# Attention ahead of two expert layers: blocks of 128 queries with both heads in turn, side work and copies from a table, routing scratch in SBUF, first operands piece by piece

## The chip, the cores and the metric

The kernel runs on one core of one Trainium2 chip. The metric is the device time in microseconds (us) of one execution; the median of three runs is given. The engines are named as in the profile: PE (TensorE; PEld is its weight load), DVE (VectorE), ACT (ScalarE), POOL (GpSimd), SP (SyncE, which here issues transfers).

## What is computed

The reference, cut: an attention in which a query sees only keys of the same hash bucket, a layer of eight experts of which each token takes two, and a dense layer.

```python
B, H, S, D = 2, 8, 768, 64
q_bucket = sum(((q @ proj) > 0) * 2 ** arange(6)); k_bucket = likewise
scores = where(q_bucket == k_bucket, q @ k.T / 8, -1e9)
x = softmax(scores) @ v                       # -> 1536 tokens x 512
noisy = x @ w_gate + log1p(exp(x @ w_noise)) * noise
two largest of noisy per token -> experts, weights = softmax of the two
out[token] += weight * (relu(x[token] @ w1[e]) @ w2[e])      # 8 experts, 512 -> 1024 -> 512
h = out @ w_in;  result = (h * sigmoid(1.702 * h)) @ w_out   # 512 -> 2048 -> 512
```

## The kernel before

Three stages follow each other: attention (with the routing of tokens worked in), the experts, the dense layer. The change touches the attention alone, which ends about where `f_tr` (L830) begins, 272.8 us into the span.

**Blocks.** Attention is 96 steps g. A step is one block of 128 queries of one head against all 768 keys. Six steps make a unit u (two heads j, three blocks c of 384 queries), two units a pair of heads n. `dec(g)` says which block a step is: up to unit 14, three blocks of head 0 and then three of head 1. A step's work is: `a_score` (L298, four matmuls into a tile s, two buffers), `a_soft` (L310 to L312, DVE takes the row maximum), `a_exp` (L321, ACT writes P), `a_trans` (L340, six PE transposes into two tiles p, then two copies p to PT, L269 on ACT or L275 on DVE), `a_av` (L351, P times V into the PSUM bank av), `a_x` (copy of av to xu) and `a_xt` (L385, L388 and the DVE operations L380 to L395: the scaled rows of tokens and the router's logits). The loop writes the score of step g+2, then the transposes of step g, then the exponential of step g+2, then a piece of `a_av` for the unit before, then the side work of the step. Every engine takes its instructions in this written order.

**Side work.** The operands of a pair of heads (u1, v1, u2, v2: a rounded part and a rest of q and k, with hash bits as extra rows) are made ahead: `a_load` (SP), `a_hash` (L191), `a_hb` (L206, L207), `a_split` (ACT L180, L185; rest on POOL, L182, L186), `a_bits` (POOL transfers). `w_load` and `w_conv` bring six weight tiles of the experts (ACT L721, POOL L729). `r_do` runs the routing of 384 tokens in small DVE operations (L429 to L486), `r_scatter` (L493, L494) writes their rows to expert order with two indirect transfers on POOL per 128 tokens. `at(g, f)` and `at_m` put each at a step by rule (every unit, every eighth step, the next free step); for the first pair `z_q`, `z_k`, `z_hash` make all operands of a head before its first score.

**What else the change touches.** `copy` chooses ACT or DVE by the running loads `la` and `ld`. The routing keeps lg, v and w0 in columns 392 to 488 of the PSUM bank av (`pt`, and `iotp`). PT of head 0 lies in two buffers of its own (PT0), that of head 1 in hh and hl, which the experts use later. The raw q and k have one buffer each. `WARM` matmuls of ones (L523) run before the first data are there.

## Time and profile before

| | |
|---|---|
| median of 3 runs | 878.44 us (878.43 to 879.76) |
| the profiled execution's own time | 880.22 us |
| its span, first to last instruction | 878.5 us |
| PE busy | 849.7 us (97%) |
| DVE, ACT, POOL busy | 528.2, 441.8, 218.4 us |
| mean granted TensorE clock | 0.996 |

The span is what the trace shows; what lies around it (1.7 us) is only in the execution's time. PE's busy time is modelled from pipelined matmuls, whose records overlap, so that a busy PE can still wait; the distance from one matmul's start to the next says more.

### The profile page before, as it was taken

Reading aid. Unit: us, or ns where it says so; the run is one execution under the profiler, and the core shown is the slowest. Engines: PE = TensorE matmul, PEld = TensorE weight load, DVE = VectorE, ACT = ScalarE, POOL = GpSimd, SP = SyncE. Lnnn points to the kernel's source line nnn. Section 1 sums busy time; section 2 is a strip of 40 time slices with the busy share of each in tenths; the row PEclk is TensorE's granted clock in tenths of the full one; section 3 lists DMA queues with packets and bytes.
Section 4 is the critical chain, followed back from the end, with each engine's and each line's share of the span. In section 5 each row is a group of like instructions: output and inputs, shape, how many; then the busy total and the mean of one; then the engine's idle time right before and its main releaser. Section 6 shows DMA issues by size and latency. Waiting matters only on the chain.

```text
span 878.5 us, 14095 instructions
## 1 busy us (share of the span) xinstructions
PE 849.7 (97%) x5409; PEld 740.5 (84%) x5409; DVE 528.2 (60%) x1082; ACT 441.8 (50%) x782; POOL 218.4 (25%) x226
## 2 busy tenths in 40 slices
PE   7899999989998999999999999999999999999997
PEld 5567666666667999999999999988899898989897
DVE  6876777877575588989898898748512121212120
ACT  5787888777663444444545443448523131414130
POOL 5241554386122100000000000006614151504040
PEclk9999999999999999999999999999999999999999
DMA  3746644573126667878878686649301010010000
GB/s 100 251 140 203 191 127 136 163 205 79 62 90 210 232 206 230 275 253 277 253 250 298 208 286 211 207 146 334 98 25 49 25 42 31 27 47 1 25 1 27
DMA packets 52376, 132.20 MB, mean 150 GB/s; under 512 B 8912, under 2 KB 11024, under 8 KB 52304
## 3 DMA queue, kind: packets, MB, share of 16 engines
q1 hardware_dynamic: 43488, 108.82, 38.1%
q0 software_dynamic: 6992, 20.37, 7.5%
q10 hardware_dynamic: 1824, 2.05, 0.8%
q8 instruction: 44, 0.72, 0.3%
q14 instruction: 28, 0.23, 0.1%
HBM read 92.05 MB, written 35.39 MB: 145 GB/s over the span
## 4 chain that ended last, share of the span: by engine, by line
PE 87%; DVE 6%; ACT 4%; DMA 1%; issue 1%; another core or an unknown queue 0%; SPq 0%; ACTq 0%; DVEq 0%
PE av L351 7%; PE s L298 6%; PE y L875 5%; PE y L877 5%; PE y L876 5%; PE g L1109 5%; PE g L1108 5%; PE g L1110 5%; PE h L851 5%; PE h L852 5%; PE h L853 5%; PE p L340 5%; PE o L1156 4%; PE o L1154 4%; PE o L1155 4%; DVE mx L310 2%
## 5 line engine op out<-in xcount | busy, mean ns | idle before, releaser
L1118 POOL TENSOR_TENSOR gl<-sg,gh 128x512 fp32r<-128x512 f32 x48 | 67.3, 1402 | 162.3 <-ACT gh L1117 162.3
L321 ACT ACTIVATE P<-s,sm 128x768 f32<-128x768 f32 x96 | 95.2, 992 | 21.9 <-DVE sm L312 16.4
L310 DVE TENSOR_REDUCE mx<-s 128x1 f32<-128x768 f32 x96 | 91.5, 953 | 20.7 <-PE s L298 20.1
L1063 POOL DMA_INDIRECT yg<-ys,ysl x24 | 24.7, 1031 | 303.9 <-issue 302.2
L298 PE MATMUL s<-v,u 76*128 76x384 f32 (+1 forms) x384 | 93.3, 365 | 5.2 <-ACT P L321 3.8
L340 PE MATMUL p<-ident,P 128*128 128x128 f32 x576 | 82.9, 278 | 7.9 <-ACT PT L269 3.2
L298 PEld LDWEIGHTS s<-v,u 76*128 76x128 f32 (+1 forms) x384 | 63.0, 191 | 30.5 <-issue 13.0
L1114 DVE TENSOR_TENSOR sg<-g,sg 128x512 f32<-128x512 f32 x48 | 33.2, 691 | 91.4 <-ACT sg L1113 87.1
L340 PEld LDWEIGHTS p<-ident,P 128*128 128x128 f32 x576 | 67.6, 141 | 18.4 <-ACT PT L269 5.6
L351 PE MATMUL av<-PT,v 128*64 128x384 f32 (+1 forms) x216 | 73.6, 470 | 2.0 <-DVE rw L431 1.5
L858 ACT ACTIVATE hh<-h 128x416 fp32r<-128x416 f32 x56 | 29.0, 518 | 72.8 <-PE h L853 72.3
L875 PE MATMUL y<-hh,wh 128*128 128x416 f32 (+1 forms) x144 | 51.2, 356 | 0.0
L877 PE MATMUL y<-hh,wl 128*128 128x416 f32 (+1 forms) x144 | 49.9, 346 | 0.0
L876 PE MATMUL y<-hl,wh 128*128 128x416 f32 (+1 forms) x144 | 49.8, 346 | 0.0
L1113 ACT ACTIVATE sg<-g 128x512 f32<-128x512 f32 x48 | 28.7, 598 | 39.5 <-PE g L1110 37.1
L351 PEld LDWEIGHTS av<-PT,v 128*64 128x64 f32 x216 | 25.9, 141 | 26.8 <-issue 22.3
L1117 ACT ACTIVATE gh<-sg 128x512 fp32r<-128x512 f32 x48 | 30.3, 630 | 31.1 <-DVE sg L1114 30.3
L269 ACT ACTIVATE PT<-p 128x384 f32<-128x384 f32 x75 | 33.3, 486 | 19.5 <-PE p L340 16.9
L859 DVE SCALAR_TENSOR_TENSOR hl<-h,hh 128x416 fp32r<-128x416 f32 x56 | 32.9, 588 | 14.2 <-ACT hh L858 14.1
L1108 PE MATMUL g<-x2h,wh 128*128 128x256 f32 x144 | 40.1, 278 | 0.7 <-ACT x2h L1092 0.7
L1109 PE MATMUL g<-x2l,wh 128*128 128x256 f32 x144 | 40.1, 278 | 0.3 <-DVE x2l L1093 0.3
L1109 PE MATMUL g<-btl,wh 128*128 128x256 f32 x144 | 40.2, 279 | 0.0
(334 smaller groups left out, 2548.2 us busy)
## 6 DMA issues: line engine op xcount, KB each, us to landing
ws<-in_w SPq DMA_DIRECT2D x40, 512.0 KB, 4.9
d_in<-in_w SPq DMA_DIRECT2D x32, 512.0 KB, 4.9
bth<-in_w SPq DMA_DIRECT2D x16, 512.0 KB, 6.3
btl<-in_w SPq DMA_DIRECT2D x16, 512.0 KB, 4.2
wd<-d_o SPq DMA_DIRECT2D x32, 256.0 KB, 3.6
xs<-xeh SPq DMA_DIRECT2D x13, 512.0 KB, 6.8
rawk<-in_kT SPq DMA_DIRECT2D x15, 384.0 KB, 5.0
rawq<-in_qT SPq DMA_DIRECT2D x14, 384.0 KB, 3.8
```

The source lines that it names most:

```text
L298: nc.tensor.matmul(ps[:, hf, :HALF], l[:kk, q0:q0 + 128], r[:kk, hf * HALF:(hf + 1) * HALF], start=st, stop=not st)
L310: nc.vector.tensor_reduce(mx, ps[:, :, :HALF], axis=AX.XY, op=ALU.max, negate=True)
L321: nc.scalar.activation(P, ps[:, :, :HALF], AF.Exp, bias=sm[:, 1:2], scale=sm[:, 0:1], accum_out=self.RS[u][:, c, j, 0:1])
L340: nc.tensor.transpose(ps[:, kb, :], P[:, hf, kb * 128:(kb + 1) * 128], self.ident)
L351: nc.tensor.matmul(self.AV[u, c][64 * j:64 * j + 64, :], self.vt[n][:, kb, 64 * j:64 * j + 64], self.PT[u, j][:, kb, cs], start=(kb == 0), ...
L851: nc.tensor.matmul(ps, wh[:, fs], xh[:, d, :n], start=(d == 0), stop=False)
L875: nc.tensor.matmul(ps, wh[:, ds_], hh[:, f, :], start=(f == 0), stop=False)
L876: nc.tensor.matmul(ps, wh[:, ds_], hl[:, f, :], start=False, stop=False)
L877: nc.tensor.matmul(ps, wl[:, ds_], hh[:, f, :], start=False, stop=(f == 7))
L1108: nc.tensor.matmul(ps[:, x, :], wh[:, fs], xh[:, d, :], start=(d == 0), stop=False)
L1109: nc.tensor.matmul(ps[:, x, :], wh[:, fs], xl[:, d, :], start=False, stop=False)
L1118: nc.gpsimd.tensor_tensor(gl[:, fo, :], g, gh[:, fo, :].bitcast(F32), op=ALU.subtract)
```

## The change

- `dec` takes the two heads of a block in turn (unit 0 has an order of its own), and `a_av` multiplies one block of 128 queries as soon as both heads are transposed: at steps 3 and 5, then at each even step. Before, it took 384 queries of both heads, two of six key blocks at a time, in the unit after. PT is now one block of both heads, alternately in hh and hl; PT0 is gone, and the raw q and k have two buffers.
- Each piece of side work has its step in a table written out; each copy has its engine in the string `COPIES` (151 on ACT and 59 on DVE, where it was 145 and 65).
- The routing's lg, v and w0 are SBUF tiles; two copies that were there to bring an operand out of PSUM or into it are gone.
- The first pair's operands are made by eight small functions from the table, the loads of k come earlier, the rest of head 0's keys (v2) is made on POOL, and 27 warm-up matmuls run instead of 40.

The diff, cut to its core (the table has some 190 rows):

```diff
-WARM = 40
+WARM = 27
...
         if n == 0:
+            raw = {(nm, j): self.t(self.ap, [128, S], F32, f"raw{nm}{j}", 2) for j in range(2) for nm in ("q", "k")}
+            nc.scalar.dma_start(raw["k", 0], a["kT"][b, 2 * p])
             nc.scalar.dma_start(self.projq, a["projq"])
-            raw = {(nm, j): self.t(self.ap, [128, S], F32, f"raw{nm}{j}", 1) for j in range(2) for nm in ("q", "k")}
-            nc.scalar.dma_start(raw["k", 0], a["kT"][b, 2 * p])
-            for nm, j, c0, c1 in (("q", 0, 0, HALF), ("q", 1, 0, HALF), ("k", 1, 0, S), ("q", 0, HALF, S), ("q", 1, HALF, S)):
+            for nm, j, c0, c1 in (("q", 0, 0, HALF), ("k", 1, 0, S), ("q", 1, 0, HALF), ("q", 0, HALF, S), ("q", 1, HALF, S)):
...
+        self.z_sub(e, v2[0:64, :], self.raw[0]["k", j][0:64, :], v1[0:64, :].bitcast(F32))
...
+    def z_bits(self, nm, j, hf):
+        nc = self.nc
+        r = 64 * (nm == "k") + 32 * j
+        d = self.uv[0, j][2 if nm == "q" else 3][64:76, hf * HALF:(hf + 1) * HALF]
+        o = nc.vector.tensor_scalar(d, self.zps[hf][r:r + 12, :], 0.0, self.sgn[r:r + 12, 0:1], op0=ALU.is_gt, op1=ALU.add)
+        self.z_other(o, r, hf, False)
+        if nm == "q":
+            nc.scalar.activation(d, d.bitcast(F32), AF.Copy, scale=BIG)
...
+    def pick(self, act, dve):
+        n = self.ncopy = self.ncopy + 1
+        return self.COPIES[n - 1:n] == "a"
+
     def copy(self, o, i, act, dve, scale=None):
-        if self.la + act <= self.ld + dve:
+        if self.pick(act, dve):
             self.la += act
             self.nc.scalar.activation(o, i, AF.Copy, scale=1.0 if scale is None else scale)
...
-        j, c = divmod(s, 3) if u < 15 else (s % 2, s // 2)
+        c, j = divmod(s, 2) if u else ((0, 0), (1, 0), (0, 1), (1, 1), (2, 0), (2, 1))[s]
...
-        if (u, j) not in self.PT:
-            if j == 0:
-                self.PT[u, j] = self.t(self.ap, [128, 6, HALF], F32, "PT0", 2)
-            else:
-                t = self.t(self.hp, [128, 8 * CAP], F32, "hl" if u % 2 else "hh", 1)
-                self.PT[u, j] = t[:, :6 * HALF].rearrange("p (k q) -> p k q", k=6)
-        PT = self.PT[u, j]
+        x = 3 * u + c
+        if j == 0:
+            t = self.t(self.hp, [128, 8 * CAP], F32, "hl" if x % 2 else "hh", 1)
...
+    def a_av(self, u, c):
+
         nc = self.nc
         n, qh = self.un(u)
-        cs = slice(0, HALF) if c is None else slice(c * 128, c * 128 + 128)
-        if kb == 0:
-            self.AV[u, c] = self.pa[:, :cs.stop - cs.start]
-        for j in range(2):
-            nc.tensor.matmul(self.AV[u, c][64 * j:64 * j + 64, :], self.vt[n][:, kb, 64 * j:64 * j + 64],
-                             self.PT[u, j][:, kb, cs], start=(kb == 0), stop=(kb == 5))
+        PT = self.PT.pop(3 * u + c)
+        for kb in range(6):
+            for j in range(2):
+                nc.tensor.matmul(self.pa[64 * j:64 * j + 64, c * 128:(c + 1) * 128],
+                                 self.vt[n][:, kb, 64 * j:64 * j + 64], PT[:, j, kb, :],
+                                 start=(kb == 0), stop=(kb == 5))
+        if u == 15:
...
-        lg, v, w0 = pt(392, 16), pt(440, 8), pt(464, 8)
+        lg, v, w0 = tt("rlg", f=16), tt("rv"), tt("rw0")
...
-            nc.vector.tensor_copy(w1, z)
-            nc.vector.scalar_tensor_tensor(w1, z, -1.0, w1, op0=ALU.mult, op1=ALU.min)
+            nc.vector.scalar_tensor_tensor(w1, z, -1.0, z, op0=ALU.mult, op1=ALU.min)
...
-            nc.vector.tensor_copy(m1, mx[:, :, 0])
-            nc.vector.tensor_tensor(m1, mx[:, :, 1], m1, op=ALU.subtract)
+            nc.vector.tensor_tensor(m1, mx[:, :, 1], mx[:, :, 0], op=ALU.subtract)
...
+            (-3, self.z_v2, 0, "p"),
...
+            (44, self.a_xt, 6),
...
+            (53, self.w_conv, 3),
...
+            (55, self.r_scatter, 0, 0),
...
+            (57, self.r_scatter, 0, 1),
...
+            (61, self.r_scatter, 0, 2),
...
+            (66, self.r_scatter, 1, 0),
...
+            (69, self.r_scatter, 1, 1),
...
+            (70, self.r_scatter, 1, 2),
...
-            if u > 0:
-                early = ((0, 1), (2, 3), (4, 5), (), (), ())
-                sp = ((), (0, 1), (), (2, 3), (), (4, 5)) if u < 14 else early
-                for kb in sp[s]:
-                    self.a_av(u - 1, kb)
-                    if kb == 5:
-                        self.a_x(u - 1)
...
+            if g in (3, 5) or g >= 6 and g % 2 == 0:
+                self.a_av(*divmod(g // 2 - 1, 3))
...
-        t = self.t(self.ap, [128, 3, DM], F32, "PT0", 2)
+        t = self.t(self.ap, [128, 3, DM], F32, "xrow0", 1)
```

How the change moves instructions, at three places. First, PE right behind the warm-up, before; m and av are the hash banks, s_2 and s_3 the scores of the first two blocks:

```order
L191 MATMUL m_1_213<-rawk0_1_107,projq_1_80 32x384
L191 MATMUL av_1_96<-rawk0_1_107,projq_1_80 32x384
L191 MATMUL m_1_213<-rawq0_1_106,projq_1_80 32x384
L191 MATMUL av_1_96<-rawq0_1_106,projq_1_80 32x384
L298 MATMUL s_2_224<-v10_1_204,u10_1_199 128x384 x2
L298 MATMUL s_2_224<-v20_1_205,u20_1_200 128x384 x2
L298 MATMUL s_3_241<-v10_1_204,u10_1_199 128x384 x2
L298 MATMUL s_3_241<-v20_1_205,u20_1_200 128x384 x2
L191 MATMUL m_2_253<-rawk1_1_109,projq_1_80 32x384
```

The same place in the change:

```order
L191 MATMUL m_1_194<-rawq0_1_105,projq_1_80 32x384
L191 MATMUL av_1_96<-rawk0_1_106,projq_1_80 32x384
L191 MATMUL m_1_194<-rawk0_1_106,projq_1_80 32x384
L191 MATMUL m_1_194<-rawk1_1_108,projq_1_80 32x384
L191 MATMUL av_1_96<-rawk1_1_108,projq_1_80 32x384
L310 MATMUL s_2_212<-v10_1_190,u10_1_185 128x384 x2
L310 MATMUL s_2_212<-v20_1_191,u20_1_186 128x384 x2
L191 MATMUL m_1_194<-rawq1_1_107,projq_1_80 32x384
L310 MATMUL s_3_230<-v10_1_190,u10_1_185 128x384 x2
L310 MATMUL s_3_230<-v20_1_191,u20_1_186 128x384 x2
L191 MATMUL av_1_96<-rawq0_1_105,projq_1_80 32x384
L310 MATMUL s_4_249<-v11_1_192,u11_1_187 128x384 x2
```

The hash of the first head's q no longer stands between the keys and the first score for both halves: its second half (av from rawq0) has moved behind the second score, and the hash of head 1's keys has moved ahead of the first.

Second, PE at the scores of steps 25 and 26 (s_27 and s_28: a score's number is its step's plus 2), before, where a piece of P times V is four matmuls of 384 queries from PT0 and hh:

```order
L298 MATMUL s_27_968<-v10_3_751,u10_3_747 128x384 x2
L298 MATMUL s_27_968<-v20_3_752,u20_3_748 128x384 x2
L340 MATMUL p_49_978<-ident_1_122,P_24_939 128x128 x3
L340 MATMUL p_50_983<-ident_1_122,P_24_939 128x128 x3
L351 MATMUL av_1_96<-PT0_3_628,v_2_499 64x384
L351 MATMUL av_1_96<-hh_2_728,v_2_499 64x384
L351 MATMUL av_1_96<-PT0_3_628,v_2_499 64x384
L351 MATMUL av_1_96<-hh_2_728,v_2_499 64x384
L298 MATMUL s_28_996<-v10_3_751,u10_3_747 128x384 x2
```

In the change, at the scores of steps 26 and 27, it is twelve of 128 from one tile:

```order
L310 MATMUL s_28_1102<-v10_3_826,u10_3_822 128x384 x2
L310 MATMUL s_28_1102<-v20_3_827,u20_3_823 128x384 x2
L350 MATMUL p_51_1113<-ident_1_122,P_25_1065 128x128 x3
L350 MATMUL p_52_1118<-ident_1_122,P_25_1065 128x128 x3
L360 MATMUL av_1_96<-hl_6_1054,v_2_390 64x128 x12
L310 MATMUL s_29_1140<-v11_3_828,u11_3_824 128x384 x2
L310 MATMUL s_29_1140<-v21_3_829,u21_3_825 128x384 x2
L350 MATMUL p_53_1150<-ident_1_122,P_26_1100 128x128 x3
L350 MATMUL p_54_1155<-ident_1_122,P_26_1100 128x128 x3
```

The pieces stand as often as before, behind the transposes of every second step, but each reads what the two steps just before it made.

Third, POOL in the first tokens' scatter (xs is the experts' buffer, xr the token rows, wl a weight's rest), before:

```order
L494 DMA xs_59<-xr_1_669,slot_1_148 15360x512
L493 MEMSET spacer_1_154 1x1
L494 DMA xs_59<-xr_1_669,slot_1_148 15360x512
L493 MEMSET spacer_1_154 1x1
L494 DMA xs_59<-xr_1_669,slot_1_148 15360x512
L493 MEMSET spacer_1_154 1x1
L494 DMA xs_59<-xr_1_669,slot_1_148 15360x512
L729 TENSOR_TENSOR wl_6_2525<-ws_6_2232,wh_6_2524 128x1024
L181 DMA u20_8_2621<-u10_8_2620 64x768
```

and in the change, from the fourth of the six indirect transfers:

```order
L504 DMA xs_59<-xr_1_536,slot_1_147 15360x512
L881 TENSOR_TENSOR wl_5_2470<-ws_5_2192,wh_5_2469 128x1024
L177 DMA u20_7_2530<-u10_7_2529 64x768
L226 TENSOR_TENSOR u10_7_2529<-rawq0_7_1858,u10_7_2529 64x768
L215 DMA u20_7_2530<-hb_6_2473 12x768
L216 DMA v20_7_2534<-hb_6_2473 12x768
L215 DMA u21_7_2532<-hb_6_2473 12x768
L216 DMA v21_7_2536<-hb_6_2473 12x768
L503 MEMSET spacer_1_153 1x1
L504 DMA xs_59<-xr_1_536,slot_1_147 15360x512
L503 MEMSET spacer_1_153 1x1
L504 DMA xs_59<-xr_1_536,slot_1_147 15360x512
```

The six transfers stood together; now four stand together, then a weight and a split, then two. The second 384 tokens' are split into two and four in the same way.

## Rows read from the trace of the kernel before

**Rows 1.** PE timeline, undisturbed steps: start us, duration us, engine, line, tiles, shape, count.

```profile
70.46 0.98 PE L298 MATMUL s<-v,u 128*128 128x384 f32 x4
...
71.85 0.94 PE L298 MATMUL s<-v,u 128*128 128x384 f32 x4
...
73.39 0.54 PE L351 MATMUL av<-PT,v 128*64 128x384 f32 x1
...
74.83 0.98 PE L298 MATMUL s<-v,u 128*128 128x384 f32 x4
```

**Rows 2.** PE timeline: an `a_xt` up to the next score, and a hash up to the next.

```profile
125.78 0.86 PE L385 MATMUL m<-wg,xu 128*128 128x32 f32 x6
...
126.75 0.95 PE L298 MATMUL s<-v,u 128*128 128x384 f32 x4
...
166.67 0.51 PE L191 MATMUL m<-rawq,projq 64*32 64x384 f32 x1
...
167.48 0.97 PE L298 MATMUL s<-v,u 128*128 128x384 f32 x4
```

**Rows 3.** PE timeline: the scores of steps 6 and 90.

```profile
23.08 0.95 PE L298 MATMUL s<-v,u 128*128 128x384 f32 x4
...
245.15 0.95 PE L298 MATMUL s<-v,u 128*128 128x384 f32 x4
```

**Rows 4.** PE timeline of the opening; in brackets the idle time before and its releaser.

```profile
8.27 0.83 PE L191 MATMUL av<-rawq,projq 64*32 64x384 f32 x2 [0.82 <-DMA rawq<-in_qT]
9.03 1.92 PE L298 MATMUL s<-v,u 128*128 128x384 f32 x8
...
18.73 1.65 PE L298 MATMUL s<-v,u 128*128 128x384 f32 x4
```

**Rows 5.** ACT, DVE and POOL timelines of the opening.

```profile
5.30 0.93 ACT L238 ACTIVATE v<-rawk,sc 128x768 fp32r<-128x768 f32 x1 [1.22 <-DMA rawk<-in_kT]
...
6.27 0.95 DVE L240 TENSOR_TENSOR v<-rawk,v 64x768 fp32r<-64x768 f32 x1 [1.60 <-ACT v L238]
7.57 0.61 DVE L255 TENSOR_SCALAR u<-m,sgn 12x384 fp32r<-12x384 f32 x1 [0.35 <-PE m L191]
...
10.43 0.96 DVE L310 TENSOR_REDUCE mx<-s 128x1 f32<-128x768 f32 x1
...
10.46 1.81 POOL L240 TENSOR_TENSOR v<-rawk,v 64x768 fp32r<-64x768 f32 x1
```

**Rows 6.** Windows of low clock: busy time (and count) by engine, PEclk, DMA share, GB/s.

```profile
17.49:20.91 3.42, 3.28 (x14) 2.56 (x13) 2.09 (x6) 3.39 (x8) 1.65 (x2) 0.50 0.02 5
266.67:270.08 3.41, 3.37 (x28) 2.64 (x26) 1.20 (x6) 0.49 (x1) 0.00 (x0) 0.50 0.84 276
```

**Rows 7.** PE timeline: a piece of twelve pairs of 128 queries, in unit 15.

```profile
261.50 0.32 PE L351 MATMUL av<-PT,v 128*64 128x128 f32 x1
...
262.96 0.88 PE L340 MATMUL p<-ident,P 128*128 128x128 f32 x6
```

**Rows 8.** PE and DVE timelines at two places where side work stands.

```profile
39.75 0.62 PE L298 MATMUL s<-v,u 76*128 76x384 f32 x2 [1.07 <-DVE v L660]
...
169.83 0.95 DVE L310 TENSOR_REDUCE mx<-s 128x1 f32<-128x768 f32 x1
```

**Rows 9.** POOL, DVE and PE timelines at the ends of two scatter runs.

```profile
193.61 0.96 POOL L494 DMA_INDIRECT xs<-xr,slot  x1 [0.22 <-issue]
...
195.68 0.56 DVE L275 COPY hl<-p 128x384 f32<-128x384 f32 x1 [2.65 <-PE s L298]
...
196.29 0.87 PE L340 MATMUL p<-ident,P 128*128 128x128 f32 x6 [2.05 <-DVE hl L275]
...
265.79 0.41 PE L385 MATMUL m<-wg,xu 128*128 128x32 f32 x2 [1.95 <-ACT xu L269]
```

**Rows 10.** Groups by line, 0 to 275 us: busy us, mean ns | idle before.

```profile
L182 POOL TENSOR_TENSOR u<-rawq,u 64x768 fp32r<-64x768 f32 x13 | 23.7, 1821 | 0.8
...
L729 POOL TENSOR_TENSOR wl<-ws,wh 128x1024 fp32r<-128x1024 f32 x6 | 14.2, 2369 | 28.1 <-ACT wh L721 21.4 <-issue 6.6
```

## What I predict, and why

> **What bounds the kernel now.** The table of the profile names PE: busy 849.7 of 878.5 us. The code behind `f_tr` is the same in both kernels, so only the first 272.8 us can move, and the question is how far PE stands above its floor there.
>
> The PE timeline gives the floor. Two undisturbed steps in a row, from a score to the score two on, take 74.83 − 70.46 = 4.37 us; the first, without a piece of P times V, takes 71.85 − 70.46 = 1.39, the second 2.98 [rows 1]. An `a_xt` adds 126.75 − 125.78 = 0.97 and a hash 167.48 − 166.67 = 0.81 [rows 2]. From the score of step 6 to that of step 90 it is 245.15 − 23.08 = 222.07 us [rows 3], for 42 pairs, 14 `a_xt` and 7 hashes: 183.5 + 13.6 + 5.7 = 202.8. The rest, 222.1 − 202.8 = **19.3 us**, is waiting of PE. What is left to win is there, in the opening and in the scatters.
>
> The chain of waits and the timelines say what PE waits for. At 39.75 it waits 1.07 us for the rest that DVE makes for pair 1 (L660) [rows 8]. Around 167 the routing, a hash and copies stand together: the score of 167.48 is done at 168.4, and DVE takes its maximum at 169.83 only [rows 2, 8]. At the end of a scatter, DVE's copy of 195.68 starts 2.07 us after the last indirect transfer (193.61) though its engine was free for 2.65, and PE loses 2.05; at the next end PE loses 1.95 [rows 9]. Two of three scatters of six transfers end between steps 6 and 90: some 4.0 of the 19.3. The other 15.3 I put down to side work standing in the way of copies, maxima and operands.
>
> In the opening PE waits 0.82 us at 8.27 for the second half of q, which stands ahead of the first score; the first score starts at 9.03 and its maximum at 10.43 [rows 4, 5]. From the first score to step 6 it is 23.08 − 9.03 = 14.05 us for six steps without a piece, whose floor is 6 × 1.39 = 8.3: 5.7 lost, in part to a stretch of 3.42 us at a granted clock of 0.50, 1.2 GHz, in which a score took 1.65 us and not 0.98 [rows 4, 6, 1].
>
> **The change part by part.**
>
> *Opening.* The wait of 0.82 and the hash of q's second half, 9.03 − 8.27 = 0.76, leave the path to the first score: 1.6 us [rows 4]. Still ahead of it are ACT's v1 (done at 6.23) and three bit operations of 0.61 on DVE, and v2 moves from DVE (0.95) to POOL (1.81 for the same shape), 0.86 longer, though beside the bit operations [rows 5]. So I expect the first maximum some 1.1 earlier, near 9.3, and the full 1.6 at step 6, since the later scores have slack. Besides, two pieces of P times V that stood behind step 90 are now done at steps 3 and 5. A piece costs 2.98 − 1.39 = 1.59; the slack of 5.7 can take both, and I count one as hidden there. Sum −1.6 − 1.6 = −3.2. Bounds: 0 (v2 on POOL, or the hash of head 1's keys now ahead of the first score, is late) and −4.8, with both pieces hidden.
>
> *Low clock.* The granted clock fell in the opening some 9 us after the wait of 0.82, and once more right behind a wait of 1.95 at a scatter's end [rows 4, 6, 9]. The first stretch, 3.42 us at half the clock, cost 1.7; the second, 3.41 us, with ACT and DVE also waiting, I put at 1.2. With 27 warm-up matmuls for 40 but a fuller first unit I take −1.0, a little over half of the first. Bounds: −2.9 (both go) and +1.7 (one more such stretch).
>
> *Pieces of P times V.* Twelve pairs of 128 queries for four of 384. The wide piece takes 74.83 − 73.39 = 1.44 us, the narrow one of unit 15 takes 262.96 − 261.50 = 1.46 [rows 1, 7]. 45 pieces by 0.02: +0.9.
>
> *Side work and copies by table.* Six copies go from DVE to ACT. That the table clears all 15.3 us is the one bound, that it clears none the other. The DVE side work to be spread is less by about two copies a routing, but the new order has tight places: xu is read by `a_xt` one step after its copy (two before), the second head's operands are wanted one step after the first head's at the start of a unit (three before), and PT of a block one step after its last copy; this last adds nothing, as p has two buffers, and the transposes of a step had to wait for the copies of the step before anyway. I take half, −7.6.
>
> *Scatters.* POOL issues as many indirect transfers, but in runs of 4, 2, 2, 4 and 6 where attention had three runs of six. What waits behind the end of a run is the copy of p, and p's transposes behind it. If the 2 us is a cost of a run, two more cost 2 × 2.0 = 4.0 [rows 9]; if of its transfers, 0. I take +2.0. If a low clock comes with each, as it did behind the third run [rows 6], it is 1.2 more for each.
>
> *Routing scratch in SBUF.* Two copies less a routing, and some ten DVE operations that now read two operands in SBUF where one was in PSUM. By themselves I cost this at nothing. POOL has, meanwhile, subtractions of 1.821 us and weight rests of 2.369 [rows 10], both reading SBUF; in the steps that the two routings fall in (45 to 63) eight and two, 8 × 1.821 + 2 × 2.369 = 19.3 us. If DVE and POOL hinder each other there, that is the bound above; nothing the bound below. The rests that DVE makes of two SBUF operands for pair 1 (L660) meet no POOL operation but transfers, and the first pair's v2 took its 0.95 with none beside it [rows 5], so rows leave it open. I take +1.0: these operations are short and off PE's path except where a copy or maximum queues behind one.
>
> The Trainium skill (SBUF — State Buffer, "Who interferes with whom") has a rule on this: a DVE instruction with two SBUF inputs and a GpSimd instruction that reads SBUF contend, and the second to issue waits until the first has ended. No row above shows the two together. By that rule the term could reach all the POOL time counted above, and the sum would end above the time before; the third rival below is that case, worked out from rows.
>
> **The sum**: −3.2 − 1.0 + 0.9 − 7.6 + 2.0 + 1.0 = −7.9. The profiled execution took 880.22, 1.78 more than the median of 878.44, so 872.3 on its scale and **870.5** on the median's.
>
> **The rivals.**
>
> *Deep.* The table clears all: −3.2 − 1.0 + 0.9 − 15.3 = −18.6, 859.8. For it: none of the 15.3 us is an engine that is full; DVE and ACT are busy 528 and 442 of 878. Against: the tight places.
>
> *No net gain.* The 14 copies of xu stand one step closer to their `a_xt`: at half an `a_xt`'s distance (0.49) each they cost 6.9 us, which eats the 7.6, 870.5 + 6.9 = 877.4. Or two further scatter ends with their low clock cost 2 × (2.05 + 1.2) = 6.5 in place of 2.0, and xu half its bound: 870.5 + 4.5 + 3.45 = 878.5. For it: PE runs at its floor in undisturbed steps, so each small lateness is paid; against: xu is one copy of 0.56 or less with a step of 1.39 at least for it.
>
> *Other side: DVE behind POOL.* In steps 45 to 63 DVE's routing operations wait for POOL's rests, and the maxima and copies queued behind them on DVE stop PE. The sum without the term of 1.0 is −8.9; the mechanism decides from 10.7 of the 19.3 us on (−8.9 + 10.7 = +1.8, the 0.2% that a measurement can tell from no change). All of it gives 878.4 − 8.9 + 19.3 = 888.8. For it: POOL's two kinds of operation last longer than a step's slack; against: most routing operations are short and few of them meet a POOL operation at its start.
>
> **How the numbers follow.** The forecast's own case holds 0.55 of the chance and lies between 865 and 875: a third or two thirds of the 15.3 (2.6 each way) and scatters at either bound (2.0 each way). Deep has 0.17, no net gain 0.16 (0.12 within 0.2%, 0.04 just faster), the other side 0.12. So faster 0.55 + 0.17 + 0.04 = 0.76, same 0.12, slower 0.12. The range leaves out most of the other side and the deepest part of deep: 859 to 879.
>
> **What would show it.** In the PE timeline: the first maximum near 9.3, step 6 near 21.5, steady pairs of 4.4 with pieces of 1.46, and step 90 some 7 us closer to step 6 than 222. PE's waits for L660 and the DVE maxima late after routing should be gone. In the scatters' stretches DVE and ACT idle some 2 us at the end of each run, or at those of three only. In steps 45 to 63 a DVE operation with two SBUF operands that takes its usual time while a POOL rest runs clears the third rival; one that ends with POOL's speaks for it. Wrong would be: PE waiting for xu ahead of each `a_xt`, a second stretch of low clock in the opening, or steady pairs over 4.5.

## The result and the profile after

The changed kernel takes **870.48 us** (median of four runs, 867.83 to 871.40) where the kernel before took 878.73: ratio 0.9899, 95% interval 0.9874 to 0.9924. A second set of runs, beside the kernel before on one chip, gave 0.9903 (0.9881 to 0.9926). The forecast was 870.5. But the terms behind it were not right: the stretch that I had expected to win a little won a lot, and the opening that I had expected to win lost.

| start of | before | changed | difference |
|---|---|---|---|
| first score | 9.03 | 7.91 | −1.12 |
| step 6 | 23.08 | 27.14 | +4.06 |
| step 90 | 245.15 | 235.23 | −9.92 |
| expert 0's transposes (`f_tr`) | 272.77 | 258.00 | −14.77 |
| last PE matmul | 873.01 | 860.50 | −12.51 |
| span | 878.5 | 867.5 | −11.0 |

So step 6 to step 90 takes 208.09 us in place of 222.07 [rows 3], and from step 90 to `f_tr` it is 22.77 in place of 27.62. In the profiled executions 3.8 us of the 14.8 are given back behind `f_tr`, in code that is the same: one stretch of low clock at 587 us in the changed kernel and an end that takes longer. The medians differ by 8.3. Some 2 us of the difference in the stretch belong to the profiled execution of the kernel before and not to its code: with edits that do not change its time by anything that can be told, it has stretches of 219.46 and 219.96 (e2 and e10 below).

The opening on PE, in the changed kernel (timeline; in brackets the idle time before and its releaser):

```profile
1.65 3.06 PE L533 MATMUL s<-ones 128*128 128x128 bf16 x27 [1.65 <-DVE ones L89]
6.46 0.81 PE L191 MATMUL m<-rawq,projq 64*32 64x384 f32 x1 [1.76 <-DMA projq<-in_projq]
...
9.36 1.13 PE L310 MATMUL s<-v,u 76*128 76x384 f32 x2 [0.44 <-DVE v L263]
...
19.09 1.65 PE L310 MATMUL s<-v,u 128*128 128x384 f32 x4
...
21.67 1.63 PE L310 MATMUL s<-v,u 128*128 128x384 f32 x4
...
27.14 0.98 PE L310 MATMUL s<-v,u 128*128 128x384 f32 x4
...
235.23 0.94 PE L310 MATMUL s<-v,u 128*128 128x384 f32 x4
```

and DVE, in the same execution:

```profile
9.77 0.62 DVE L263 TENSOR_SCALAR v<-m,sgn 12x384 fp32r<-12x384 f32 x1
10.32 0.61 DVE L263 TENSOR_SCALAR v<-av,sgn 12x384 fp32r<-12x384 f32 x1
10.97 0.96 DVE L322 TENSOR_REDUCE mx<-s 128x1 f32<-128x768 f32 x1
```

The PE lines answer to [rows 3, 4]. The 27 warm-up matmuls end at 4.71, and PE idles 1.76 us until the hash matrix is there. From then on a score takes 1.65 us, the length that it had inside the stretch of 0.50 in the kernel before [rows 4, 6], up to the one at 21.67: PE runs at 1.2 GHz for some 16 us. (The windows view of this execution prints a clock of 1.00 there, because its first clock record comes at 24 us; the durations tell it.) Before, the low stretch was 3.42 us. The wait for q's second half is gone as forecast, but the score's second half then waits for the hash bits of the keys, and the first maximum starts at 10.97 where it was 10.43 [rows 5], not at 9.3. Five bit operations stand ahead of it on DVE, one behind the other from 7.96 to 10.93; the last two, shown above, are for the keys of head 1.

Groups by line of 0 to 275 us: the PE lines of the changed kernel, and under them those of the kernel before (busy, mean ns | idle before, releasers):

```profile
L310 PE MATMUL s<-v,u 76*128 76x384 f32 (+1 forms) x384 | 96.4, 374 | 0.5 <-DVE v L263 0.4
L350 PE MATMUL p<-ident,P 128*128 128x128 f32 x576 | 81.4, 277 | 1.2 <-ACT hh L281 1.0 <-DVE hh L287 0.2
L398 PE MATMUL m<-wg,xu 128*128 128x32 f32 x94 | 12.4, 267 | 0.0
```

```profile
L298 PE MATMUL s<-v,u 76*128 76x384 f32 (+1 forms) x384 | 93.3, 365 | 5.2 <-ACT P L321 3.8 <-DVE v L660 1.1
L340 PE MATMUL p<-ident,P 128*128 128x128 f32 x576 | 82.9, 278 | 7.9 <-ACT PT L269 3.2 <-DVE hl L275 2.5 <-DVE PT L275 1.0
L351 PE MATMUL av<-PT,v 128*64 128x384 f32 (+1 forms) x216 | 73.6, 470 | 2.0 <-DVE rw L431 1.5 <-ACT xu L269 0.4
L385 PE MATMUL m<-wg,xu 128*128 128x32 f32 x94 | 13.3, 277 | 1.9 <-ACT xu L269 1.9
```

The waits of scores and transposes fall from 13.1 to 1.7 us, and no `a_xt` (L398) ever waits for its xu, though it follows the copy one step closer. A line that I should have read in the kernel before is the third: P times V waits 1.5 us for DVE's L431, a routing operation whose operands lie in PE's bank av.

A quiet pair of steps in the changed kernel, with an `a_xt` in it (PE timeline):

```profile
212.93 1.53 PE L360 MATMUL av<-hh,v 128*64 128x128 f32 x24
214.39 0.98 PE L310 MATMUL s<-v,u 128*128 128x384 f32 x4
...
215.86 0.75 PE L398 MATMUL m<-wg,xu 128*128 128x32 f32 x6
...
219.73 0.98 PE L310 MATMUL s<-v,u 128*128 128x384 f32 x4
```

The narrow piece takes 214.39 − 212.93 = 1.46 us, as in [rows 7]. The pair takes 219.73 − 214.39 = 5.34, which without the `a_xt` (0.95 here) is 4.39 against 4.37 [rows 1].

### The profile page after: what moved, and what is told of

It reads as the page before. It is cut to its first block, busy times and chain, and to the rows that moved or that the text cites. A ratio compares the mean times of both kernels' runs of the same rounds, so it can differ in the third digit from the quotient of the medians.

```text
span 867.5 us, 15549 instructions
## 1 busy us (share of the span) xinstructions
PE 849.0 (98%) x6116; PEld 779.3 (90%) x6116; DVE 525.0 (61%) x1066; ACT 444.4 (51%) x788; POOL 221.3 (26%) x227
## 4 chain that ended last, share of the span: by engine, by line
PE 72%; DMA 2%; POOL 2%; DVE 1%; ACT 1%; issue 1%; ACTq 0%; DVEq 0%; POOLq 0%
PE y L1029 5%; PE y L1027 5%; PE y L1028 5%; PE h L1003 5%; PE h L1004 5%; PE h L1005 5%; PE g L1260 5%; PE g L1261 5%; PE g L1262 5%; PE o L1308 4%; PE o L1306 4%; PE o L1307 4%; PE av L360 2%; PE s L310 2%; PE p L350 2%; DMA w3l<-wd 1%
## 5 line engine op out<-in xcount | busy, mean ns | idle before, releaser
L310 PE MATMUL s<-v,u 76*128 76x384 f32 (+1 forms) x384 | 96.4, 374 | 0.5 <-DVE v L263 0.4
L310 PEld LDWEIGHTS s<-v,u 76*128 76x128 f32 (+1 forms) x384 | 65.0, 196 | 17.3 <-issue 11.9
L350 PEld LDWEIGHTS p<-ident,P 128*128 128x128 f32 x576 | 70.0, 143 | 7.2 <-ACT hh L281 1.8
L1262 PE MATMUL g<-x2h,wl 128*128 128x256 f32 x144 | 40.5, 281 | 0.0
L1260 PE MATMUL g<-bth,wh 128*128 128x256 f32 x144 | 40.1, 279 | 0.0
L1262 PE MATMUL g<-bth,wl 128*128 128x256 f32 x144 | 40.1, 278 | 0.0
```

The costliest lines, as they stand in the source:

```text
L310: nc.tensor.matmul(ps[:, hf, :HALF], l[:kk, q0:q0 + 128], r[:kk, hf * HALF:(hf + 1) * HALF], start=st, stop=not st)
L350: nc.tensor.transpose(ps[:, kb, :], P[:, hf, kb * 128:(kb + 1) * 128], self.ident)
L1260: nc.tensor.matmul(ps[:, x, :], wh[:, fs], xh[:, d, :], start=(d == 0), stop=False)
L1262: nc.tensor.matmul(ps[:, x, :], wl[:, fs], xh[:, d, :], start=False, stop=(d == 3))
```

## The experiments

"Stretch" is the time from the score of step 6 to that of step 90 in each profiled execution; ratios are to the kernel before on the same chip. The changed kernel has 0.9899 and 0.9903, and a stretch of 208.1 in both of its profiles.

| run | ratio, 95% interval | median us | step 6 at | stretch |
|---|---|---|---|---|
| e1_warm40 | 0.9848 (0.9828 to 0.9867) | 863.89 | 24.03 | 208.08 |
| e2_before_warm27 | 1.0002 (0.9988 to 1.0016) | 877.77 | 23.35 | 219.46 |
| e3_copies_by_load | 0.9943 (0.9925 to 0.9961) | 872.35 | 27.41 | 213.22 |
| e4_scatters_bunched | 1.0002 (0.9989 to 1.0014) | 877.20 | 26.98 | 220.68 |
| e5_after_psum_scratch | 0.9927 (0.9904 to 0.9951) | 877.21 | 25.84 | 216.48 |
| e6_before_sbuf_scratch | 1.0017 (0.9995 to 1.0039) | 884.42 | 22.87 | 225.28 |
| e7_order_without_table | 1.0215 (1.0181 to 1.0249) | 902.69 | 27.13 | 240.28 |
| e8_scatters_bunched_early | 1.0000 (0.9980 to 1.0020) | 884.58 | 25.86 | 222.77 |
| e9_changed_again | 0.9903 (0.9881 to 0.9926) | 868.93 | 27.05 | 208.11 |
| e10_before_scatters_apart | 1.0006 (0.9993 to 1.0020) | 877.69 | 22.96 | 219.96 |
| e11_warm40_projq_first | 0.9854 (0.9831 to 0.9877) | 865.58 | 25.91 | 208.13 |
| e12_warm40_fill | 0.9865 (0.9842 to 0.9888) | 865.97 | 25.06 | 208.06 |

The kernel before had medians of 877.9, 883.1 and 877.3 us on the three chips (e1 to e4, e5 to e8, e9 to e12), so medians are compared within those groups only.

**The opening: 40 warm-up matmuls in the changed kernel (e1).**

```diff
-WARM = 27
+WARM = 40
```

> The changed kernel with 40 warm-up matmuls again in place of 27, nothing else. Theory (clock): in the changed kernel PE works at half speed from its first hash at 6.46 to 24.06 us, because its warm-up ends 1.76 us before the first data; with 40 it runs into them, the full clock comes near 7.3 us as in the kernel before, a score takes 0.95 and not 1.65 us from then on, and step 6 starts at 21 to 23.5 us in place of 27.1: 864 to 867.5 us. Rival (chain): the opening is set by the chain of DVE, POOL and ACT operations for the first scores, and PE's speed is hidden behind it: step 6 at 26 to 27 us, 869.5 to 871.5 us.

Measured: ratio 0.9848, which is 0.0051 or 4.5 us under the changed kernel's first set, and a median just under the range of the theory; step 6 at 24.03, 3.1 us earlier, slightly later than the range that I gave. The opening on PE, and the windows view of it (busy time and count by engine, PEclk, DMA share, GB/s):

```profile
6.38 0.71 PE L191 MATMUL m<-rawq,projq 64*32 64x384 f32 x1 [0.28 <-DMA projq<-in_projq]
...
8.86 0.88 PE L310 MATMUL s<-v,u 76*128 76x384 f32 x2 [0.87 <-DVE v L263]
...
10.52 1.65 PE L310 MATMUL s<-v,u 128*128 128x384 f32 x4
...
17.47 0.97 PE L310 MATMUL s<-v,u 128*128 128x384 f32 x4
```

```profile
7.40:10.20 2.80, 1.90 (x11) 0.78 (x6) 2.68 (x5) 1.45 (x2) 2.72 (x3) 1.00 0.67 80
10.30:17.10 6.80, 6.80 (x19) 3.88 (x18) 5.32 (x13) 4.29 (x9) 2.02 (x2) 0.50 0.80 316
17.20:23.00 5.80, 5.33 (x40) 4.35 (x40) 4.99 (x12) 4.56 (x9) 1.53 (x2) 1.00 0.34 111
```

The warm-up now runs nearly into the first hash, the clock is at 1.00 for the first score, then at 0.50 from 10.3 to 17.1, and PE spends about 7 us at half the clock in place of 16. The theory holds in part: the gain is there, but it had the full clock last from then on, and the clock fell again. Its edit has the lowest ratio of the study.

**The same edit the other way in the kernel before (e2).**

```diff
-WARM = 40
+WARM = 27
```

> The kernel before with 27 warm-up matmuls in place of 40, nothing else. Theory (clock): its warm-up then ends before its first data too, the first record of full clock moves from 7.25 us to 20 us or later, and step 6 comes 2 to 5 us later than 23.1: 880.5 to 884 us. Rival (chain): its opening waits for DVE and ACT most of the time anyway, and step 6 moves by under 1 us: 878 to 879.7 us.

Measured: no change (1.0002), step 6 at 23.35. A miss for the clock theory as I wrote it. In this execution the first data came at 5.41, 0.70 us after the warm-up, and a full clock was granted right then. So the number 27 alone is not what costs. The idle time between the warm-up and the first data is a candidate, as the kernel before asks for the hash matrix first and has its first hash operands earlier; it is not shown to be the cause. Seven profiles have the changed opening with 27. In five (the changed kernel twice, e3, e4, e7; idle 1.34 to 1.76 us) the full clock comes only at 22.6 to 24.2. In two (e5 and e8; idle 1.45 and 1.63 us) it is there from 5.3 to 8.7, and step 6 starts at 25.84 and 25.86.

**The hash matrix first, with 40 (e11), and matmuls in the gap of the first score, with 40 (e12).**

```diff
+            nc.scalar.dma_start(self.projq, a["projq"])
             nc.scalar.dma_start(raw["k", 0], a["kT"][b, 2 * p])
-            nc.scalar.dma_start(self.projq, a["projq"])
```

> The changed kernel with 40 warm-up matmuls and the load of the hash matrix ahead of the first keys again. Theory (the idle time ahead of the first hash comes from this load): the first hash starts before 6.1 us and the 0.28 us of waiting is gone, step 6 at 23 to 24 us, ratio 0.983 to 0.985. Rival (the keys are then late): the rounded keys of head 0 and with them the first score move back by 0.3 to 1 us, ratio 0.985 to 0.987.

```diff
         for (l, r, kk, st) in ((u1, v1, 128, True), (u2, v2, K2, False)):
+            if g == 0 and not st:
+                fill = self.t(self.ps_p, [128, 3, 128], F32, "p")
+                for i in range(14):
+                    nc.tensor.matmul(fill[:, 0, :], self.ones, self.ones, start=True, stop=True)
```

> The changed kernel with 40 warm-up matmuls and 14 more matmuls of ones between the two halves of the first score, where PE waited 0.87 us for the hash bits and the granted clock fell 0.6 us after it. Theory (that wait is what made the clock fall): no stretch of 0.50 between 8 and 20 us, the six scores of the opening at 0.95 us, step 6 at 21 to 22.5 us, ratio 0.9815 to 0.9835. Rival (it falls anyway, or the chain of DVE and ACT then sets the pace): step 6 at 23.5 to 24.5, ratio 0.984 to 0.986.

Measured: 0.9854 and 0.9865, neither to be told from e1. In e11 the idle time ahead of the first hash is gone and the first score starts at 6.79, but its second half then waits 1.20 us, until POOL has made the rest of the keys (releaser L226), the clock falls at 9.3 and stays at 0.50 until 23.0, and step 6 comes at 25.91, later than the theory said. The ratio lies in the rival's range, but its mechanism, a later first score, did not come. In e12 the wait at 8.86 is filled and the clock holds until 14.0, but then PE waits 0.93 us at 13.21 for another score, and the clock falls there. Step 6 at 25.06 lies behind both ranges. In both runs one wait is closed and the clock falls behind the next one of about 1 us. That the wait makes it fall is not shown; which waits it takes, and why the fall lasts 3.4, 6.8 or 13.7 us in these openings, stays open.

**Copies by load (e3).**

```diff
     def pick(self, act, dve):
-        n = self.ncopy = self.ncopy + 1
-        return self.COPIES[n - 1:n] == "a"
+        return self.la + act <= self.ld + dve
```

> The changed kernel with the rule of before for the engine of each copy (the running loads of ACT and DVE) in place of the written string; order and table stay. Theory (the written order and table removed the waits, the string adds little): 870 to 872 us, the stretch from step 6 to step 90 within 2 us of 208.1. Rival (the string is what keeps copies on time): the stretch grows by 4 to 10 us, 874 to 880 us.

Measured: ratio 0.9943, so 3.9 us slower than the changed kernel's set; stretch 213.22, 5.1 longer. The time is just above the range of the theory, the stretch within that of the rival: the string is worth 4 to 5 us. PE's waits at the transposes go from 1.2 to 3.9 us (groups by line):

```profile
L349 PE MATMUL p<-ident,P 128*128 128x128 f32 x576 | 82.8, 278 | 3.9 <-DVE hl L286 1.6 <-ACT hh L280 1.1 <-DVE hh L286 0.8
```

**The order without its table (e7).** Side work of steps 3 to 84 by the rules of the kernel before, copies by load.

```diff
-            (5, self.a_hash, 1),
...
-            (79, self.a_xt, 12),
...
+        for n in range(1, NP):
+            g = {1: 7, 2: 15, 3: 29, 4: 40, 5: 50, 6: 60, 7: 71}[n]
...
+        xt = [self.at_m(73 if u == 9 else 6 * u + 13, self.a_xt, u) for u in range(12)]
```

> The changed kernel (blocks with both heads in turn, its opening, scratch in SBUF) with the side work from step 3 to 84 put by the rules of the kernel before and copies by load. With the copies by load alone the ratio was 0.9943. Theory (the table is half of the gain): the stretch from step 6 to step 90 lies between 213 and 222 us, ratio 0.996 to 1.003. Rival 1 (the order of blocks does it all): ratio 0.992 to 0.996. Rival 2 (the order has so little slack that without its table it is worse than the old order): over 222 us there, ratio over 1.003.

Measured: ratio 1.0215, stretch 240.28: rival 2. Against e3 the table, which also places the scatters, is worth 27 us of stretch, and with the old rules the stretch of the new order is 18 us longer than that of the old [rows 3]. PE waits at the start of units, for operands of the first head (46.24) and, the tight place that the prediction had named, of the second (52.59). PE timeline:

```profile
46.24 0.76 PE L309 MATMUL s<-v,u 76*128 76x384 f32 x2 [3.01 <-DMA u<-u]
52.59 0.62 PE L309 MATMUL s<-v,u 76*128 76x384 f32 x2 [1.19 <-POOL v L226]
```

The longest single wait has another source, the one that the prediction's third rival had named (POOL, DVE and PE timelines):

```profile
192.37 2.38 POOL L758 TENSOR_TENSOR wl<-ws,wh 128x1024 fp32r<-128x1024 f32 x1
192.47 2.32 DVE L447 TENSOR_TENSOR rw<-rv,nz 128x24 f32<-128x24 f32 x1
...
194.71 1.79 POOL L226 TENSOR_TENSOR v<-rawk,v 64x768 fp32r<-64x768 f32 x1
194.82 1.72 DVE L448 TENSOR_TENSOR rw<-rlg,rw 128x24 f32<-128x24 f32 x1
...
198.57 1.54 PE L349 MATMUL p<-ident,P 128*128 128x128 f32 x6 [3.73 <-DVE hl L286]
```

The two routing operations take 0.18 us each in the changed kernel. Here each ends 0.04 us after POOL's rest beside it; the maximum behind them starts at 196.80, the copy at 197.97, and PE waits 3.73. So the table also keeps routing and rests apart.

**Routing scratch back in PSUM (e5), and into SBUF in the kernel before (e6).** e6 is the same edit with + and − exchanged.

```diff
-        lg, v, w0 = tt("rlg", f=16), tt("rv"), tt("rw0")
+        pt = lambda o, f: self.pa[:, o:o + 3 * f].rearrange("p (i f) -> p i f", f=f)[:, :n, :]
+        lg, v, w0 = pt(392, 16), pt(440, 8), pt(464, 8)
...
+            nc.vector.tensor_copy(w1, z)
-            nc.vector.scalar_tensor_tensor(w1, z, -1.0, z, op0=ALU.mult, op1=ALU.min)
+            nc.vector.scalar_tensor_tensor(w1, z, -1.0, w1, op0=ALU.mult, op1=ALU.min)
```

> The changed kernel with the routing's lg, v, w0 and the row of numbers back in PSUM and the two copies a routing back; all else as changed. In the trace of the changed kernel DVE operations with two SBUF operands take 1334 ns instead of 202 (the product with the one-hot rows) or 848 instead of 157 when a POOL rest runs at their start. Theory A (the lock is real but hidden): these long ones vanish, PE does not notice, and the ratio to the kernel before stays within 0.002 of the changed kernel's 0.990. Rival B (the lock reaches PE): 1.5 to 4 us come back, ratio 0.9855 to 0.988.

> The kernel before with the routing's scratch in SBUF and the two copies a routing left out, nothing else. Theory A (hidden): ratio 0.998 to 1.002, with single DVE operations of 0.8 to 2 us beside POOL rests in the trace. Rival B (the lock reaches PE where the order is not made for it): 1.5 to 5 us slower, ratio 1.002 to 1.006.

Measured, e5: 0.9927, just beyond what A allows and on the other side from rival B; the intervals of e5 and the changed kernel overlap, so that a loss is not shown, though the stretch is 8.4 us longer. What neither theory had is in e5's timelines (POOL, DVE and PE): pieces of P times V wait for routing operations whose operands lie in the same bank, and PE waits 2.36 us at the end of a run of four indirect transfers.

```profile
159.86 0.97 POOL L509 DMA_INDIRECT xs<-xr,slot  x1 [0.23 <-issue]
160.24 0.26 DVE L444 TENSOR_REDUCE av<-lg 128x48 f32<-128x96 f32 x1 [3.00 <-PE s L312]
...
162.28 1.52 PE L352 MATMUL p<-ident,P 128*128 128x128 f32 x6 [2.36 <-ACT hh L283]
...
181.78 1.53 PE L362 MATMUL av<-hl,v 128*64 128x128 f32 x24 [1.20 <-DVE wgt L501]
...
239.48 1.53 PE L362 MATMUL av<-hh,v 128*64 128x128 f32 x24 [0.49 <-DVE rw L446]
...
263.19 1.53 PE L362 MATMUL av<-hh,v 128*64 128x128 f32 x24 [1.36 <-DVE wgt L501]
```

Step by step against the changed kernel, 4.2 of the 8.4 us lie at the wait of 162 and 2.4 at the end of the other run of four (199 to 207). The three steps with waits on the bank (0.59 at 130.84, 1.20 and 0.49) are 2.5 longer in all, and 0.7 is won elsewhere. The runs of four stand in the changed kernel too, without such waits; it was not run on this chip.

e6: 1.0017 (0.9995 to 1.0039), in the range of A, with an interval that reaches into that of B, and not to be told from no change. Its trace has the DVE operations that wait (DVE and POOL timelines):

```profile
153.42 1.83 POOL L180 TENSOR_TENSOR u<-rawq,u 64x768 fp32r<-64x768 f32 x1
...
153.94 1.36 DVE L432 SCALAR_TENSOR_TENSOR rv<-rlg,rw 128x24 f32<-128x24 f32 x1
...
155.33 2.40 POOL L724 TENSOR_TENSOR wl<-ws,wh 128x1024 fp32r<-128x1024 f32 x1
155.54 2.22 DVE L434 TENSOR_TENSOR rw<-rlg,rw 128x24 f32<-128x24 f32 x1
```

They end at 155.30 and 157.76, POOL's at 155.25 and 157.73. A copy stands behind the second, and PE waits 0.93 us for it at 159.79.

**Scatters in one run each (e4, e8), and apart in the kernel before (e10).**

```diff
-            (55, self.r_scatter, 0, 0),
...
             (65, self.a_xt, 9),
+            (65, self.r_scatter, 0, 0),
+            (65, self.r_scatter, 0, 1),
+            (65, self.r_scatter, 0, 2),
...
+            (75, self.r_scatter, 1, 0),
```

> The changed kernel with the scatters of the first and the second 384 tokens each as one run of six again (at steps 65 and 75). In the changed kernel none of the run ends shows a wait of PE of 2 us. Theory (a long run is what costs, by its end): the two runs bring back 1.5 to 4 us in all, 872 to 874.5 us, with a wait of ACT or DVE near the last indirect transfer of each. Rival (the waits of before came from where its copies stood, not from the run): within 1 us, 869.5 to 871.5 us.

Measured: ratio 1.0002, 9 us slower than the changed kernel, against 1.5 to 4 expected. But the place was a bad one: a DVE write of the next rows (`a_xt` of unit 9, L408) stood behind the transfers that read the same buffer and DVE was idle 8.34 us. And with the transfers gone from their old place, POOL's rests met the routing: a DVE operation of 0.20 us (L496) took 1.64 beside one, and PE waited 2.04 at 183.59. The second run, at 221 to 228 us, delayed nothing: the six steps around it took 14.11 us, as in the changed kernel. So it was run again ahead of that write:

```diff
             (55, self.r_scatter, 0, 0),
+            (55, self.r_scatter, 0, 1),
+            (55, self.r_scatter, 0, 2),
...
-            (57, self.r_scatter, 0, 1),
...
             (66, self.r_scatter, 1, 0),
+            (66, self.r_scatter, 1, 1),
+            (66, self.r_scatter, 1, 2),
```

> The changed kernel with the first two scatters as one run of six each, but at steps 55 and 66, ahead of the rows that are written into the same buffer (in the run before at step 65 such a write waited 8.34 us for the transfers). Theory (the length of a run costs nothing, what counts is who waits for the rows): ratio within 0.002 of the changed kernel's 0.990, no wait of PE over 0.6 us near the two ends. Rival (each end of a long run costs some 2 us, as the profile before was read): ratio 0.993 to 0.996 and waits of 1.5 to 2 us near the ends.

Measured: ratio 1.0000, again 9 us, more than the rival said. DVE, ACT, PE and POOL at the end of its first run (timeline):

```profile
159.03 0.94 PE L310 MATMUL s<-v,u 128*128 128x384 f32 x4
...
162.08 0.97 POOL L504 DMA_INDIRECT xs<-xr,slot  x1 [0.22 <-issue]
162.85 0.96 DVE L322 TENSOR_REDUCE mx<-s 128x1 f32<-128x768 f32 x1 [4.98 <-remote]
...
164.26 0.87 ACT L281 ACTIVATE hh<-p 128x384 f32<-128x384 f32 x2 [5.23 <-remote]
...
164.81 1.54 PE L350 MATMUL p<-ident,P 128*128 128x128 f32 x6 [4.84 <-ACT hh L281]
```

The score was done at 159.97, and DVE took its maximum at 162.85, after the sixth transfer, with nothing else to do for 4.98 us. The same stands at the end of the second run (PE waits 2.50), and each is followed by a granted clock of 0.50. The changed kernel has nothing of it: its first run of four ends at 161.72, DVE takes maxima at 159.87 and 161.99, and PE does not wait. Between the runs of e8 stands what e4 had: L496 takes 1.63, PE waits 2.11 at 188.89, and a low clock follows. Step by step, 7.0 us of the 14.7 that its stretch is longer lie at the first end, 4.4 at the second, and 4.0 at this place between them (0.7 is won elsewhere).

```diff
-                self.at(max(g + 2, sc) + i, self.r_scatter, bq, i)
+                self.at(max(g + 2, sc) + 3 * i, self.r_scatter, bq, i)
```

> The kernel before with the three pairs of indirect transfers of a scatter three steps apart in place of one (steps 64, 67, 70 and 75, 78, 81), nothing else. Theory (a run of six delays whatever waits for PE near its end, in the old order too): the waits of 2.05 us at 196 goes, 1 to 4 us come back, ratio 0.9955 to 0.999. Rival (only the new order, with its copies one step closer, is hurt by a long run): ratio 0.999 to 1.001.

Measured: 1.0006, the rival. But the edit did less than it was to do: in the trace the first scatter is a run of four and one of two, and the second still a run of six, from 213.98 to 221.35, as POOL came to it late. And e2, whose runs of six are those of the kernel before, shows none of the waits of [rows 9] at their ends: its stretch is 219.46, that of e10 219.96, where the profiled execution of the kernel before had 222.07. Step by step, that execution loses 1.7 us against e2 at the first end and 1.1 at the second.

Over all 14 profiles, such idle time (DVE or ACT near the end of a run, with what they take long done) stands in five: the kernel before and e5 to e8, which ran on one chip. It comes there at runs of six and, in e5, at runs of four. The other nine, on the two other chips or of the changed kernel's first set, have none, though all have a run of six. So no run shows a price of a run's length; the waits go with the execution or the chip.

**The changed kernel again (e9).** The same file.

> The changed kernel itself once more, beside the three that follow, since kernels of different calls ran on different chips. If the chip doesn't matter to the comparison, its ratio to the kernel before is 0.988 to 0.992; and the scatter runs of two and four again show no wait of PE over 0.6 us.

Measured: 0.9903, stretch 208.11, no wait of PE over 0.48 us in it, as expected.

## Why the prediction came out as it did

The number was right; the sum behind it was not. Two errors of opposite sign cancelled.

*Opening, −3.2, and low clock, −1.0.* Both signs were wrong: step 6 came 4.06 later in place of 1.6 earlier. Of this 1.5 is the piece that now stands ahead of step 6, which I had counted as hidden, and 3.1 the warm-up, by e1. The prediction had named a second stretch of low clock in the opening as a sign of being wrong; what came is one stretch, but of some 16 us in place of 3.42. The step that failed is "27 warm-up matmuls for 40 but a fuller first unit": I asked how full PE is after its first data, and not what it does in the microseconds ahead of them. The bound of +1.7 (one more stretch as in [rows 6]) was too small as well. The first maximum did not move to 9.3, since the chain of hash bits on DVE, and not the wait for q's second half, sets it: I had counted three bit operations, and the two for head 1's keys now stand ahead of it as well. With 40 warm-up matmuls the chain still sets it (10.47 in e1).

*Pieces, +0.9.* Right: 1.46 for 1.44 and a pair of 4.39 for 4.37.

*Side work and copies, −7.6, scatters, +2.0, port, +1.0.* Together −4.6; measured is −14.0 − 0.8 = −14.8 in the stretch (the 0.8 are the 42 pieces there), or some −12 against the stretches of e2 and e10, in which the waits of [rows 9] did not come. My half was the wrong half: some three quarters of the 19.3 us went, and nearly all of the idle time that scores and transposes had, as in the rival called deep. The tight places that I set against it are real (e7: +27 us without the table, in part by routing behind POOL), but the table serves each of them.

*Scatters.* I read the wait at a run's end as a price of each run, so that more runs cost more. It is not one: the changed kernel's five runs show none, its run of six included, e5's runs of four do, and three runs of six in e2 do not. The 4.0 us that I took out of the 19.3 for two ends were 2.8 in that execution, step by step against e2, and nothing in e2; the 1.95 that I called the next end is the third run's, behind step 90. What e4 and e8 lose is not the length of the runs alone: e4 has a write that waits for the transfers, e8 the waits that came on its chip with runs of four as well, and both have routing behind POOL. Whether splitting wins anything in the old order is open, as e10 split one scatter of two and ran where no such wait was seen.

*Scratch in SBUF.* The third rival's mechanism is there. In the changed kernel (POOL and DVE timelines):

```profile
173.29 1.82 POOL L226 TENSOR_TENSOR u<-rawq,u 64x768 fp32r<-64x768 f32 x1
...
173.85 1.33 DVE L481 TENSOR_TENSOR pw<-oh,rw 128x48 f32<-128x48 f32 x1
...
175.22 0.20 DVE L483 TENSOR_REDUCE slot<-pw 128x6 int32<-128x48 f32 x1
```

The product takes 0.20 us when no POOL rest runs and 1.33 here; it ends at 175.18, POOL's rest at 175.11. The Trainium skill's rule (SBUF — State Buffer, "Who interferes with whom"), by which a DVE instruction with two SBUF inputs and a GpSimd instruction that reads SBUF block each other until the first is done, agrees with these rows and with those of e6. PE does not wait for it in the changed kernel, so the term of +1.0 came to nothing there. That is the work of the table: with routing and rests otherwise placed, PE waited 3.73 us (e7), 2.04 (e4), 2.11 (e8) and 0.93 (e6). The edit also has a gain that I had costed at nothing: it takes the routing out of PE's bank av. That wait was in the trace of before (1.5 us, L431), and with the new order it would be 3.6 us at four places (e5: 0.59 + 1.20 + 0.49 + 1.36). In the time this gain is not shown, since the intervals overlap.

*xu one step ahead of its* `a_xt` *(6.9 at most).* Nothing: the idle time before L398 is 0.0 in 94 matmuls.

*Behind step 90,* −4.85 for the −1.6 of one piece: the waits of 1.95 and the low clock of [rows 6, 9] did not come, and a new wait of 1.68 for the first expert's rows took some of it.

Where parts are undone singly, the losses (4 for the copies, 9 for the scatters in their two wrong places, over 20 for the table; 2 for the scratch, not clear of noise) add up to far more than the whole change gains. They are not terms of one sum: the new order with the old rules costs some 18 us of stretch, and the parts together pay for that and for the gain. The −8.3 us of the medians are that net, with 3 to 4.5 us left behind in the warm-up.

## What to carry to other kernels

- A sum can hit for wrong reasons: check the terms at milestones (here step 6, step 90, the end of the stage) before the forecast is called understood.
- A wait that is seen in one profiled execution is not yet a price. Look for the same place in other executions of the same code, on another chip too, before it is multiplied by a count; and look for who shares a PSUM bank with PE before moving scratch is costed at nothing.
- Fewer warm-up matmuls are no saving when PE then idles until the first operands land: here 40 in place of 27 won 0.5% in the changed kernel and nothing in the kernel before. Try the number anew when the opening changes.
- A wait that a trace doesn't show may be kept away by the written order alone. When one piece of side work is moved, look at what then stands beside it on the other engines.

## What the runs showed of the hardware

- PE's clock after 1.76 us of idle time behind the warm-up was low for some 16 us (a score at 1.65 us until 21.67, at 0.94 from 24.14); with 0.28 us of idle time a full clock came first and a stretch of 0.50 of 6.8 us later. With the same 27 warm-up matmuls and 1.45 and 1.63 us of idle time (e5, e8) it was granted in full from 5.3 to 8.7 and then 0.50 for 13.7 us; e7, on the chip of these two, with 1.59 us, had the full clock only at 22.6. So neither the idle time nor the chip decides alone. Where a low stretch followed a full clock in these openings, it was 3.4, 6.8 or 13.7 us long.
- DVE and ACT can stand idle for up to some 5 us near the end of a run of indirect transfers although PE's result is done (159.97 against 162.85 in e8). It came in the profiles of the kernel before and of e5 to e8, at runs of four (e5) and six, and in none of the nine others, with runs of six as well. In the same five the DMA view has no time to landing for the scatters' transfers; in the other nine it has 2.7 to 5.5 us. What decides it stays open.
- A DVE operation of 0.2 us with two SBUF operands that meets a POOL rest ends 0.03 to 0.07 us after it, in all five cases shown here (1.33, 1.36, 1.72, 2.22 and 2.32 us).
